# Two more landing places in ring slots, and a seventh product half a step earlier, in a spectral MLP kernel

## The chip, the cores and the metric

The kernel runs on one core of a Trainium2 chip. Its engines work in parallel, each through its own row of instructions in order, and wait for each other through semaphores: TensorE (PE in the profile, its weight loads PEld) multiplies, VectorE (DVE) and ScalarE (ACT) work element by element, GpSimd (POOL) does a few small powers, SyncE (SP) issues the transfers between the chip's main memory and on-chip memory. The metric is device time in microseconds (us) of one execution; the median of three runs is given. Below the chip is told only as the profile shows it.

## The reference

Two layers, each an FNet mixing (a Fourier transform over the hidden and the sequence axis, real part kept) and a spatial-shift MLP. S = 2048, D = 512, F = 1376, all float32:

```
def _A_ref(x, dft_seq_re, dft_seq_im, dft_hid_re, dft_hid_im):
    a = jnp.einsum("bsd,ed->bse", x, dft_hid_re)
    b = jnp.einsum("bsd,ed->bse", x, dft_hid_im)
    return jnp.einsum("ts,bse->bte", dft_seq_re, a) - jnp.einsum("ts,bse->bte", dft_seq_im, b)

def _B_ref(x, w1, w2, w3, w4):
    h = _gelu(_layernorm(x, axis=-1) @ w1)
    ...                                  # four column groups shifted by +1, -1, +2, -2 rows
    x1 = x + hs                          # hs: the shifted h @ w2
    return x1 + _gelu(_layernorm(x1, axis=-1) @ w3) @ w4

x = x + _A_ref(_layernorm(x, axis=-1), ...)
x = x + _B_ref(_layernorm(x, axis=-1), ...)
x = x + _A_ref(_layernorm(x, axis=-1), ...)      # layer 1 from here
x = x + _B_ref(_layernorm(x, axis=-1), ...)
```

## The kernel before

Every product of float32 matrices is made of three TensorE products of a high and a low part of each operand (mm3, lines 343 to 345: high by high, high by low, low by high). So every operand must be split: ScalarE casts a high part, VectorE subtracts it from the source to get the low part.

The transform over the sequence is done in four chunks c of 512 rows. Each chunk has an **x phase** and a **y phase** of eight blocks k. An x phase has 16 half-steps: in half-step 2k the block of the sequence matrix "plain k" is multiplied into the PSUM banks PC and PB (two banks, "a pair", each), in half-step 2k + 1 "half k" (one 128x512 part: the difference of the two rows of the same block) into PA. A y phase has for each k an item "by1" (into PC and PD) and one "by0" (into PB and PA). What a chunk leaves is copied out of PSUM and then multiplied with the hidden transform's matrices.

In layer 1 that second multiplication, for chunk c - 1, is spread over the x phase of chunk c (c = 1, 2, 3) as **seven products of half-size matrices, forms 0 to 6**, in place of eight (hid7). The left operands are sums of the four quarters (a11 ... a22 in the tiles imL, reL, s2, s3), split into a high part in one of two buffers hf[n % 2] (form_high, ScalarE, line 490) and a low part written in place (form_low, VectorE, line 494). The right operands are two blocks for each form, ready-made in main memory (hsd). The table HAT7 says in which half-step each form's products run: 5, 10, 11, 12, 13, 14, 15. Form n accumulates in PD[n % 2], and forms 0, 1, 3 and 6 start it anew. hid7_out adds what stands in PD to the result tiles (VectorE, line 567, the rows with "psd"), at the first half-step after the form's own, in form_outs; form 4 is added to two column halves at once (128x1024), the others are 128x512. So form 6, which starts PD[0] anew, needs form 4's sum to be done, and PD's first product of the y phase needs those of forms 5 and 6. The sums and splits of the left operands are hung on half-steps in the table "late" at the end of y_phase.

**How operands come in.** A list of *pieces* (transfers of 512 KB) is issued in order on SP's queue by issue_dma, each as soon as a *raw place* is free: four places, and two more (raw 4 and 5) for pieces of y phases and, in layer 1, of all that ahead_pieces lists. ahead_pieces sorts the pieces by the half-step in which they are due; a form's two are due one half-step ahead of it. A list of *items* is worked on in two stages by prefetch: stage one makes the difference where one is needed (VectorE, lines 281 and 285) and the high part (ScalarE, lines 279, 282, 286) in one of four slots of a *ring*, stage two the low part (VectorE, line 300). A form's item takes no slot: its products read the raw place. Stage one runs ahead of the products as far as slots are free and pieces are issued, in the order of the list, and stops at the first item whose piece has no place. The program is recorded in exactly the order in which these functions are called, so a place more shifts where an item's instructions stand on VectorE and ScalarE, relative to the forms' work and the rest.

A slot holds high and low parts of two rows (2 x 2 x 512 words). An item "half" uses the first row only, so in layer 1's x phases with c > 0, where odd slots hold "half" items, the second halves of slots 1 and 3 are unused.

**Beside it** a unit of layer 1's w4 is prepared in each x phase (w4_sums): loaded at half-step 2, four sums of 128x256 on VectorE and a cast on ScalarE at half-step 13, the low part and the transfer out to main memory at half-step 15.

The page's names: ring0f to ring3f are the differences in the four slots, imL and reL the forms' low parts, hf the high parts, rawr a form's block in its raw place, tmp the result tiles.

Of the kernel before, what the change touches and what calls it, by code (L numbers as in the profile page):

```python
# [8 lines left out]
F32 = mybir.dt.float32  # L9
# [10 lines left out]
CH = 512  # L20
# [3 lines left out]
DH = D // 2  # L24
# [14 lines left out]
BACK = {8: 0, 11: 2, 13: 4}  # L39
HORDER = ((1, 0), (0, 1), (1, 1), (0, 0))  # L40
XLEAD, YLEAD = 4.5, 3.5
HAT7 = (5, 10, 11, 12, 13, 14, 15)


@with_exitstack
def spectral_mlp_kernel(ctx: ExitStack, tc: tile.TileContext, x, ws, hs, w1, w2, w34, out):
# [41 lines left out]
    def at(name, word, *shape, dtype=F32R):  # L88
        return nc.alloc_sbuf_tensor_at(name, [P, *shape], dtype, offset=base + 4 * word).ap()
# [23 lines left out]
    raw_at += [at(f"raw{RAW + i}", word, 2, CH, dtype=F32) for i, word in enumerate((EXT + 4 * D, STG))]  # L113
    raw_in = [RAWS + i * 2 * CH for i in range(RAW)] + [EXT + 4 * D, STG]
    raw_in = [at(f"rawr{i}", word, 2, 2, DH) for i, word in enumerate(raw_in)]

    blk, blkf = {}, {}
    for i, word in (("11", H3), ("21", H3 + 4 * CH), ("12", RNG), ("22", RNG + 4 * CH)):
# [34 lines left out]
        return tmps[(count["tmp"] - 1) % len(tmps)]  # L153


    pieces, items, w_items, w_pieces, y_pieces = [], [], [], [], set()

    def piece(src, a=0, b=2):
        pieces.append((src, a, b))
# [10 lines left out]
    def ahead_pieces(c):  # L170
        order = [(2 * k - XLEAD, 0, (k,), ws[c, k][:, 2:4]) for k in range(NP)]
        order += [(t - 1, j, (h, j), hsd[h][j]) for h, t in enumerate(HAT7) for j in range(2)]
        for k in range(NP):
            order += [(2 * NP + 2 * k - YLEAD, i, (k, "y", i), ws[c, k][:, 2 - 2 * i : 4 - 2 * i]) for i in range(2)]
        order.sort(key=lambda o: o[:2])
        ids = {name: piece(src) for _, _, name, src in order}
        y_pieces.update(ids.values())
        return ids

    def form_items(step, ids):  # L180
# [5 lines left out]
    for layer in range(LAYERS):  # L186
        for c in range(NC):
            if layer == 0 and c == 0:
                for k in range(NP):
                    item("plain", piece(ws[c, k][:, 2:4]))  # L190
                    item("plain", piece(ws[c, k][:, 0:2]))
                continue
            if c and layer:
                ids = ahead_pieces(c)
                for k in range(NP):
                    form_items(2 * k, ids)
                    item("plain", ids[(k,)])
                    form_items(2 * k + 1, ids)
                    item("one", ids[(k,)], span=(0, 1))
                for k, kind in y_order():  # L200
                    item(kind, ids[k, "y", 0], ids[k, "y", 1])
                continue
            for k in range(NP):
                if c:
                    for h in range(NP):
                        if HAT[h] == k:
                            item("plain", piece(hs[HORDER[h % 4]]))
                p = piece(ws[c, k][:, 2:4])
                item("plain", p)
                item("one", p, span=(0, 1))  # L210
            ps = [(piece(ws[c, k][:, 2:4]), piece(ws[c, k][:, 0:2])) for k in range(NP)]
            y_pieces.update(i for p in ps for i in p)
            for k, kind in y_order():
                item(kind, *ps[k])
        for o in HORDER:
            item("plain", piece(hs[o]))
        w_items.append(len(items))
        for i in range(2):
            item("plain", piece(w1[i]), dest=w12[i])
        for i in range(2):  # L220
            item("plain", piece(w2[i]), dest=w12[2 + i])
        w_pieces.append(len(pieces))
# [18 lines left out]
    def issue_dma(upto=None):  # L241
        while state["dma"] < (state["load"] if upto is None else upto):
            i = state["dma"]
            free = [
                r
                for r, p in held.items()
                if (r < RAW or state["wide"] and i in y_pieces)
                and (p is None or all(n < state[stage] for n, stage in uses[p]))
            ]
            if not free:  # L250
                break
            src, a, b = pieces[i]
            r = min(free, key=lambda r: (-1 if held[r] is None else held[r], r))
            held[r] = i
            raws[i], place[i] = raw_at[r], r
            if uses[i][0][1] == "over":
                raws[i] = raw_in[r].bitcast(F32).rearrange("p i l w -> p i (l w)")
            nc.sync.dma_start(raws[i][:, a:b], src)
            state["dma"] += 1
            if i % 2 and i > 3:  # L260
                load_x()

    def stage_one():

        n = state["one"]
        kind, ids, (a, b), dest = items[n]
        issue_dma()
        if kind == "form":
            state["one"] += 1
            return  # L270
        if dest is None:
            dest = ring[state["made"] % RING]
            sums[n] = ringf[state["made"] % RING][:, :, 1]
            state["made"] += 1
        slots[n] = dest
        r = [raws[i] for i in ids]
        lo = sums.get(n)
        if kind == "plain":
            nc.scalar.copy(dest[:, a:b, 0], r[0][:, a:b])  # L279
        elif kind == "one":  # L280
            nc.vector.tensor_tensor(lo[:, 0], r[0][:, 1], r[0][:, 0], op=ALU.subtract)
            nc.scalar.copy(dest[:, 0, 0], lo[:, 0])  # L282
        else:
            i = 1 if kind == "by1" else 0
            nc.vector.tensor_tensor(lo, r[1][:, i : i + 1].broadcast_to([P, 2, CH]), r[0], op=ALU.subtract)  # L285
            nc.scalar.copy(dest[:, :, 0], lo)  # L286
        state["one"] += 1
        issue_dma()
# [285 lines left out]
    def x_phase(c, hook, seven=False, tiles=0):  # L574
# [2 lines left out]
        ready = []  # L577

        def form_steps(step):
            if seven and step in HAT7:  # L580
                ready.append(HAT7.index(step))
                hid7(ready[-1])

        def form_outs(step):
            while ready and HAT7[ready[0]] < step:
# [34 lines left out]
    def y_phase(c, hook, tiles=0):  # L620
# [32 lines left out]
        if tiles:  # L653
            for i, f in (
# [17 lines left out]
                (11, lambda: form_high(4)),  # L672
                (12, lambda: form_low(4)),
                (12, lambda: form_high(5)),
                (13, lambda: form_low(5)),
                (13, lambda: form_high(6)),
                (14, lambda: form_low(6)),
            ):
                late.setdefault(i, []).append(f)
            return  # L680
# [1188 lines left out]
    def w4_sums(k, i):  # L1869

        if i == 2:
            w4_bring(k)
        if i == (13 if layer else 10):
            w4_raw = w4_sumf[:, :, 0].rearrange("p (f h) w -> p h f w", f=2)
            a, b = (w4_raw[:, h] for h in range(2))
            s = w4_sumf[:, :, 1]
            add(s[:, 0], b[:, 0], b[:, 1])
            add(s[:, 1], s[:, 0], a[:, 0], ALU.subtract)
            add(s[:, 2], a[:, 0], b[:, 0], ALU.subtract)
            add(s[:, 3], a[:, 1], s[:, 1], ALU.subtract)  # L1880
            nc.scalar.copy(w4_sum[:, :, 0], s)
        if i == (15 if layer else 11):
            nc.vector.tensor_tensor(
                w4_sum[:, :, 1], w4_sumf[:, :, 1], w4_sum[:, :, 0].bitcast(F32), op=ALU.subtract
            )
            nc.sync.dma_start(w4s[k], w4_sum.bitcast(F32))
# [273 lines left out]
```

## Time and profile before

| | |
|---|---|
| runs | 1452.15, 1454.65, 1456.01 us; median 1454.65 |
| profiled execution | 1454.98 us, span of the instructions 1452.9 us |
| TensorE | busy 1420.9 us (98%), granted clock 0.996 on average |
| VectorE | busy 1204.9 us (83%) |
| ScalarE | busy 731.8 us (50%) |
| transfers | 324.05 MB on SP's queue, 66.9% of the 16 engines' time |

Busy time of TensorE is modelled and overlaps from one product to the next, so 98% does not mean that nothing can be gained; what can be seen is where it stands still, and what ended each such wait. In the part with layer 1's x phases c = 1 to 3 (780 to 1110 us from the start) the named waits of TensorE add up to 17.9 us. In a timeline each row has start and duration in us, engine, line, operation, the tile written and the tiles read, shapes and a count; a wait stands in brackets with what ended it.

### The profile page before, as it was taken

The page shows a single profiled execution, that of the slowest core. Times are in us where ns is not written, and L with a number is a line of the kernel's source. Part 1 is how long each engine was busy: PE and PEld are TensorE (multiplying, and loading weights), DVE is VectorE, ACT ScalarE, POOL GpSimd, SP SyncE. Part 2 cuts the span into 40 slices and gives each one's busy share as a digit, 9 for nine tenths or more (in the row PEclk, how much of TensorE's full clock was granted, in tenths as well). Part 3 has the DMA queues.
Part 4 walks back from the last instruction along what each step waited for, and adds up shares of the span by engine and source line. Part 5 has one row for each costly group of instructions (what it writes and reads, how often), then busy time and mean ns, then how long its engine had stood idle before and what let it go on. Part 6 is the DMA issues. An engine that isn't in the chain of part 4 may idle for free.

```text
span 1452.9 us, 18506 instructions
## 1 busy us (share of the span) xinstructions
PE 1420.9 (98%) x6681; PEld 1188.4 (82%) x6681; DVE 1204.9 (83%) x1725; ACT 731.8 (50%) x1020; POOL 76.6 (5%) x105
## 2 busy tenths in 40 slices
PE   9999999999999999998999989989989999999999
PEld 7888888888888888876888878878878888899887
DVE  7986998989978897667799878879879797897676
ACT  5663554445566654344555443444445666444342
POOL 2100000000002000000000000000000011000000
PEclk9999999999999999999999999999999999999999
DMA  7867657568645758877655577576687537586864
GB/s 247 274 204 234 200 173 261 173 200 296 226 133 161 268 214 282 329 251 263 232 173 190 203 256 225 187 269 222 207 294 240 173 102 275 165 250 217 320 205 163
DMA packets 145628, 325.24 MB, mean 224 GB/s; under 512 B 10624, under 2 KB 61568, under 8 KB 142848
## 3 DMA queue, kind: packets, MB, share of 16 engines
q1 hardware_dynamic: 145536, 324.05, 66.9%
q8 instruction: 53, 0.87, 0.2%
q14 instruction: 39, 0.32, 0.1%
HBM read 262.41 MB, written 61.60 MB: 223 GB/s over the span
## 4 chain that ended last, share of the span: by engine, by line
PE 83%; DVE 9%; DMA 4%; ACT 2%; issue 2%; SPq 0%; DVEq 0%; ACTq 0%
PE psd L343 8%; PE psd L345 8%; PE psd L344 8%; PE psa L343 7%; PE psa L344 7%; PE psa L345 7%; PE psb L344 6%; PE psb L343 6%; PE psb L345 6%; PE psc L344 6%; PE psc L345 6%; PE psc L343 6%; DVE ring L300 1%; DVE rest L567 1%; DMA raw<-in_ws 1%
## 5 line engine op out<-in xcount | busy, mean ns | idle before, releaser
L300 DVE TENSOR_TENSOR ring<-raw,ring 128x1024 fp32r<-128x1024 f32 x102 | 124.2, 1220 | 19.0 <-ACT ring L279 18.7
L279 ACT CAST ring<-raw 128x1024 fp32r<-128x1024 f32 x103 | 107.8, 1051 | 56.3 <-PE psd L345 25.6
L383 POOL TENSOR_TENSOR rs<-ve,mhalf 128x4 f32<-128x4 f32 x16 | 25.0, 1562 | 746.1 <-DVE nm L382 746.1
L343 PE MATMUL psd<-ring,ay 128*128 128x512 f32 x126 | 50.1, 398 | 7.8 <-DVE tmp L567 7.8
L300 DVE TENSOR_TENSOR ring<-ring1f,ring 128x512 fp32r<-128x512 f32 (+1 forms) x56 | 53.3, 952 | 2.9 <-ACT ring L282 2.9
L286 ACT CAST ring<-ring0f 128x1024 fp32r<-128x1024 f32 x28 | 29.5, 1053 | 50.5 <-DVE ring0f L285 50.2
L286 ACT CAST ring<-ring2f 128x1024 fp32r<-128x1024 f32 x28 | 29.6, 1056 | 48.8 <-DVE ring2f L285 48.8
L343 PE MATMUL psd<-rawr,hf 128*128 128x256 f32 x168 | 47.7, 284 | 5.8 <-issue 4.8
L343 PE MATMUL psc<-ring,ay 128*128 128x512 f32 x128 | 50.2, 392 | 2.0 <-ACT rr11f L608 1.7
L300 DVE TENSOR_TENSOR ring<-ring3f,ring 128x1024 fp32r<-128x1024 f32 (+1 forms) x50 | 49.3, 986 | 3.0 <-ACT ring L282 2.6
L362 POOL TENSOR_TENSOR rs<-ve,mhalf 128x2 f32<-128x2 f32 (+2 forms) x33 | 29.2, 886 | 426.6 <-DVE nb L361 407.6
L391 ACT ACTIVATE tmp<-xs,nb,rs 128x512 f32<-128x512 f32 x56 | 43.3, 810 | 15.8 <-POOL nb L363 12.6
L344 PE MATMUL psb<-ring,ay 128*128 128x512 f32 x128 | 50.3, 393 | 0.8 <-DVE ring L300 0.8
L343 PE MATMUL psb<-ring,ay 128*128 128x512 f32 x128 | 50.5, 394 | 0.0
L345 PE MATMUL psb<-ring,ay 128*128 128x512 f32 x128 | 50.1, 391 | 0.0
L345 PE MATMUL psd<-ring,ay 128*128 128x512 f32 x126 | 49.9, 396 | 0.0
L344 PE MATMUL psc<-ring,ay 128*128 128x512 f32 x128 | 49.8, 389 | 0.0
L345 PE MATMUL psc<-ring,ay 128*128 128x512 f32 x128 | 49.8, 389 | 0.0
L344 PE MATMUL psd<-ring,ay 128*128 128x512 f32 x126 | 49.8, 395 | 0.0
L344 PE MATMUL psa<-ring,ay 128*128 128x512 f32 x126 | 49.0, 389 | 0.0
L343 PE MATMUL psa<-ring,ay 128*128 128x512 f32 x126 | 49.0, 389 | 0.0
L345 PE MATMUL psa<-ring,ay 128*128 128x512 f32 x126 | 49.0, 389 | 0.0
(896 smaller groups left out, 4757.8 us busy)
## 6 DMA issues: line engine op xcount, KB each, us to landing
raw<-in_ws SPq DMA_DIRECT2D x183, 512.0 KB, 5.2
w4r<-w4d SPq DMA_DIRECT2D x44, 512.0 KB, 5.3
rawr<-hsd SPq DMA_DIRECT2D x42, 512.0 KB, 4.8
w3b<-w3d SPq DMA_DIRECT2D x10, 1792.0 KB, 9.3
raw<-in_hs SPq DMA_DIRECT2D x32, 512.0 KB, 4.0
w3d<-w3b SPq DMA_DIRECT2D x5, 1792.0 KB, 7.0
hsd<-hp SPq DMA_DIRECT2D x28, 256.0 KB, 2.4
x1d<-tmp SPq DMA_DIRECT2D x12, 512.0 KB, 7.4
```

Of the source, the lines that this page charges most:

```text
L279: nc.scalar.copy(dest[:, a:b, 0], r[0][:, a:b])
L286: nc.scalar.copy(dest[:, :, 0], lo)
L300: nc.vector.tensor_tensor(lo, src, hi.bitcast(F32), op=ALU.subtract)
L343: nc.tensor.matmul(o, lh, rh, start=first, stop=False, skip_group_check=more)
L344: nc.tensor.matmul(o, lh, rl, start=False, stop=False, skip_group_check=more)
L345: nc.tensor.matmul(o, ll, rh, start=False, stop=last, skip_group_check=more)
L362: nc.gpsimd.tensor_tensor(rs[:, :n], ve[:, :n], mhalf[:, 0, :n], op=ALU.pow)
L383: nc.gpsimd.tensor_tensor(rs, ve, mhalf[:, :, :2], op=ALU.pow)
L391: nc.scalar.activation(o, s, AF.Identity, bias=mr[2], scale=mr[1])
L567: nc.vector.tensor_tensor(o, a, b, op=op)
```

## The change

Five edits, all for layer 1's x phases with c > 0:

- Two raw places more (6 and 7): the unused halves of ring slots 1 and 3. Items "one" of these phases become "half" and get a tile of half the size, so that the rest of the slot is free. The two places take only blocks of forms whose half-step is below 13 (forms 0 to 3), and only after the first item of the phase has been used.
- HAT7's last entry: form 6's products run in half-step 14, directly after form 5's, and its two pieces are due at 13 with form 5's.
- form_steps takes the forms of one half-step in turn, and before a form's products it records the sum of a form that stands two back (form 4 before form 6).
- The left operand of form 6 is made in half-step 13: high part, then form 5's low part, then form 6's low part.
- w4's sums and cast move from half-step 13 to 14.

```diff
-HAT7 = (5, 10, 11, 12, 13, 14, 15)
+HAT7 = (5, 10, 11, 12, 13, 14, 14)
...
+    half_in = {i: both(f"ringh{i}", RNG + i * 4 * CH, 1, 2, CH) for i in (1, 3)}
+    raw_in += [at(f"rawr{RAW + 2 + i // 2}", RNG + i * 4 * CH + 2 * CH, 2, 2, DH) for i in (1, 3)]
+    raw_at += [raw_in[RAW + 2 + i].bitcast(F32).rearrange("p i l w -> p i (l w)") for i in range(2)]
...
+        early_pieces.update((ids[h, j], len(items)) for h in range(7) for j in range(2) if HAT7[h] < 13)
...
-                    item("one", ids[(k,)], span=(0, 1))
+                    item("half", ids[(k,)], span=(0, 1))
...
-                if (r < RAW or state["wide"] and i in y_pieces)
+                if (r < RAW or state["wide"] and (i in y_pieces if r < RAW + 2 else state["use"] > early_pieces.get(i, len(items))))
...
             if uses[i][0][1] == "over":
-                raws[i] = raw_in[r].bitcast(F32).rearrange("p i l w -> p i (l w)")
+                raws[i] = raw_at[r] if r > RAW + 1 else raw_in[r].bitcast(F32).rearrange("p i l w -> p i (l w)")
...
+            if kind == "half":
+                dest, whole = half_in[state["made"] % RING]
+                sums[n] = whole[:, :, 1]
...
-        elif kind == "one":
+        elif kind in ("one", "half"):
...
         def form_steps(step):
-            if seven and step in HAT7:
-                ready.append(HAT7.index(step))
-                hid7(ready[-1])
+            for h in range(7):
+                if seven and HAT7[h] == step:
+                    while ready and ready[0] < h - 1:
+                        hid7_out(ready.pop(0))
+                    ready.append(h)
+                    hid7(h)
...
                 (12, lambda: form_high(5)),
+                (13, lambda: form_high(6)),
                 (13, lambda: form_low(5)),
-                (13, lambda: form_high(6)),
-                (14, lambda: form_low(6)),
+                (13, lambda: form_low(6)),
...
-        if i == (13 if layer else 10):
+        if i == (14 if layer else 10):
```

How it moves the instructions. **VectorE, half-steps 9 and 10 of the x phase c = 1** (s2f and imLf are the forms' left operands, reL form 1's low part, s form 2's, ring3f and ring_206 or ringh_222 the half of k = 5 and its low part). Before:

```order
L567 TENSOR_TENSOR s2f<-reLf,s3f 128x1024
L567 TENSOR_TENSOR imLf<-imLf,reLf 128x4x256
L494 TENSOR_TENSOR reL<-reLf,hf_191 128x4x256
L567 TENSOR_TENSOR imLf<-reLf,s2f 128x4x256
L494 TENSOR_TENSOR s_186<-s2f,hf_190 128x1024
L281 TENSOR_TENSOR ring3f<-raw_209 128x512
L300 TENSOR_TENSOR ring_206<-ring3f,ring_206 128x512
```

and now:

```order
L574 TENSOR_TENSOR s2f<-reLf,s3f 128x1024
L288 TENSOR_TENSOR ringh3f<-raw_209 128x512
L307 TENSOR_TENSOR ringh_222<-ringh3f,ringh_222 128x512
L574 TENSOR_TENSOR imLf<-imLf,reLf 128x4x256
L501 TENSOR_TENSOR reL<-reLf,hf_191 128x4x256
L574 TENSOR_TENSOR imLf<-reLf,s2f 128x4x256
L501 TENSOR_TENSOR s_186<-s2f,hf_190 128x1024
```

The half of k = 5 and its low part have moved from behind form 2's low part to ahead of form 1's.

**VectorE, half-steps 13 to 15** (imL is form 5's low part, reL form 6's; psd_287 and psd_293 are PD[1], read for form 3's sum, psd_286 and psd_292 PD[0], read for form 4's; the first row before is the low part of plain 7, ring3f its half, ring0f and ring1f the y phase's first two items). Before:

```order
L300 TENSOR_TENSOR ring_204<-raw_213,ring_204 128x2x512
L494 TENSOR_TENSOR imL<-imLf,hf_191 128x4x256
L567 TENSOR_TENSOR w4sumf<-w4sumf 128x256 x4
L567 TENSOR_TENSOR tmp<-tmp,psd_287 128x2x256
L281 TENSOR_TENSOR ring3f<-raw_213 128x512
L285 TENSOR_TENSOR ring0f<-raw_209,raw_210 128x2x512
L300 TENSOR_TENSOR ring_206<-ring3f,ring_206 128x512
L285 TENSOR_TENSOR ring1f<-raw_209,raw_210 128x2x512
L300 TENSOR_TENSOR ring_200<-ring0f,ring_200 128x2x512
L300 TENSOR_TENSOR ring_202<-ring1f,ring_202 128x2x512
L494 TENSOR_TENSOR reL<-reLf,hf_190 128x4x256
L567 TENSOR_TENSOR tmp<-tmp,psd_286 128x1024
```

and now:

```order
L501 TENSOR_TENSOR imL<-imLf,hf_191 128x4x256
L501 TENSOR_TENSOR reL<-reLf,hf_190 128x4x256
L574 TENSOR_TENSOR tmp<-tmp,psd_293 128x2x256
L288 TENSOR_TENSOR ringh3f<-raw_211 128x512
L307 TENSOR_TENSOR ring_204<-raw_211,ring_204 128x2x512
L292 TENSOR_TENSOR ring0f<-raw_208,raw_210 128x2x512
L307 TENSOR_TENSOR ringh_222<-ringh3f,ringh_222 128x512
L292 TENSOR_TENSOR ring1f<-raw_208,raw_210 128x2x512
L307 TENSOR_TENSOR ring_200<-ring0f,ring_200 128x2x512
L574 TENSOR_TENSOR tmp<-tmp,psd_292 128x1024
L307 TENSOR_TENSOR ring_202<-ring1f,ring_202 128x2x512
L574 TENSOR_TENSOR w4sumf<-w4sumf 128x256 x4
```

Form 6's low part has moved from near the end to directly behind form 5's, plain 7's low part from the front to behind the half, and w4's sums and the low part of the y phase's second item from ahead of form 4's sum to behind it. Behind these rows both have ring2f, w4's low part, the statistics (c = 1 and 2) and the sums of forms 5 and 6; before, ring2f's low part stood among them too, and now it comes later.

**TensorE, the first products of form 6** (rawr is the form's block; in brackets what the instruction waits for). Before, behind the last PB product of k = 7:

```order
L343 MATMUL psb_283<-ring_204,ax_152 128x512
L344 MATMUL psb_283<-ring_204,ax_152 128x512
L345 MATMUL psb_283<-ring_204,ax_152 128x512
L343 MATMUL psd_286<-rawr_217,hf_190 128x256 [waits DMAHW5_49,DVE_49,Activation_49]
L344 MATMUL psd_286<-rawr_217,hf_190 128x256
```

and now, behind the last product of form 5:

```order
L352 MATMUL psd_293<-rawr_219,imL 128x256
L350 MATMUL psd_293<-rawr_219,hf_191 128x256
L351 MATMUL psd_293<-rawr_219,hf_191 128x256
L352 MATMUL psd_293<-rawr_219,imL 128x256
L350 MATMUL psd_292<-rawr_218,hf_190 128x256 [waits DMAHW4_49,DVE_49,Activation_49]
```

The PC and PB products of k = 7 now come behind form 6's, and its first product waits for a transfer, VectorE and ScalarE as before.

More of the change, by code (lines that the diff above doesn't have):

```diff
@@ L153, in tmp_tile @@
         return tmps[(count["tmp"] - 1) % len(tmps)]
-    pieces, items, w_items, w_pieces, y_pieces = [], [], [], [], set()
+    pieces, items, w_items, w_pieces, y_pieces, early_pieces = [], [], [], [], set(), {}
     def piece(src, a=0, b=2):
```

## The prediction

> **What bounds the kernel now.** I read the chain of waits first, then what TensorE waited for in the stretch that the change touches (layer 1, x phases of c = 1, 2, 3, 780 to 1110 us), then the timelines of TensorE, VectorE and ScalarE around each of these waits.
>
> ```profile
> PE 83%; DVE 9%; DMA 4%; ACT 2%; issue 2%; SPq 0%; DVEq 0%; ACTq 0%
> ```
>
> TensorE sets the end for 83% of the span. So what counts is each stretch in which it stands still, and an edit away from it costs or gains only through such a stretch. In the touched part there are these (engine, line, what ended the wait, us in total, times, longest):
>
> ```profile
> PE psd L343 <- DVE tmp L567: 7.8, 3, 3.2
> PE psd L343 <- issue: 4.8, 3, 2.0
> ...
> PE psd L345 <- DVE reL L494: 1.6, 3, 0.6
> ```
>
> Each comes once per phase. The columns below are start, duration, engine, line, operation, count, and in brackets the idle time before it:
>
> ```profile
> 857.15 0.40 PE L343 MATMUL psc<-ring,ax 128*128 128x512 f32 x1
> ...
> 862.05 0.36 PE L343 MATMUL psd<-rawr,hf 128*128 128x256 f32 x1 [2.00 <-issue]
> ...
> 865.00 0.40 PE L343 MATMUL psa<-ring,ax 128*128 128x512 f32 x1
> ...
> 871.62 0.80 PE L343 MATMUL psd<-ring,ay 128*128 128x512 f32 x1 [3.19 <-DVE tmp L567]
> ```
>
> 857.15 is the last PC/PB pair of half-step 14; 862.05 is form 6 (the seventh) in half-step 15; 865.00 the last PA pair; 871.62 the y phase's first product into PD. Two VectorE rows say what the two waits are:
>
> ```profile
> 860.74 1.21 DVE L567 TENSOR_TENSOR tmp<-tmp,psd 128x1024 f32<-128x1024 f32 x1
> ...
> 870.29 1.28 DVE L567 TENSOR_TENSOR tmp<-tmp,psd 128x512 f32<-128x512 f32 x2
> ```
>
> The 128x1024 add is the sum that takes form 4 out of PD[0] (hid7_out(4)); it ends at 861.95, and form 6, which starts PD[0] anew, begins 0.10 later. So the wait marked "issue" is for form 4's sum. The second row takes forms 5 and 6 out; it ends at 871.57, and PD's first y product follows. Phase c = 2 has the same pair:
>
> ```profile
> 965.72 1.22 DVE L567 TENSOR_TENSOR tmp<-tmp,psd 128x1024 f32<-128x1024 f32 x1
> 967.04 0.36 PE L343 MATMUL psd<-rawr,hf 128*128 128x256 f32 x1 [2.00 <-issue]
> ```
>
> Both waits are thus for VectorE's place in its own row of work, not for blocks from memory.
>
> **The change, first place: half-step 9 to 10.** Two more places let the items be staged earlier, so the half of block k = 5 (ringh3f and its low part) now stands on VectorE ahead of the low part of form 1, which TensorE already waits for:
>
> ```profile
> 826.00 0.69 DVE L281 TENSOR_TENSOR ring1f<-raw 128x512 f32<-128x512 f32 x1
> 827.43 0.69 DVE L300 TENSOR_TENSOR ring<-ring1f,ring 128x512 fp32r<-128x512 f32 x1 [0.74 <-ACT ring L282]
> ...
> 832.05 1.22 DVE L567 TENSOR_TENSOR imLf<-imLf,reLf 128x1024 f32<-128x1024 f32 x1
> 833.37 1.23 DVE L494 TENSOR_TENSOR reL<-reLf,hf 128x1024 fp32r<-128x1024 f32 x1
> ...
> 834.65 0.39 PE L345 MATMUL psd<-rawr,reL 128*128 128x256 f32 x1 [0.55 <-DVE reL L494]
> ```
>
> A half and its low part, back to back, cost 1.43 from start to start (826.00 to 827.43, ScalarE's cast between them) and 0.60 for the low part itself (the same operation, 855.52 to 856.12 below). So imLf moves from 832.05 to 834.08, form 1's low part from 833.37 to 835.40, and TensorE, which follows it without slack, waits 2.03 longer. Bounds: 0 if some slack hides it (none shows: there is a 0.55 wait already), 2.03 if none. I take 2.03, three times: **+6.1**. Later rows of VectorE do not give it back, since the next waits hang on TensorE's own form 4.
>
> **Second place: half-steps 13 to 15.** I count from T, ScalarE's cast of form 6's high part, which starts as form 4's last product reads that buffer:
>
> ```profile
> 843.14 1.05 ACT L490 CAST hf<-s3f 128x1024 fp32r<-128x1024 f32 x1 [1.18 <-PE psd L344]
> ...
> 852.97 1.05 ACT L490 CAST hf<-reLf 128x1024 fp32r<-128x1024 f32 x1 [3.62 <-PE psd L344]
> ```
>
> ```profile
> 844.22 1.23 DVE L494 TENSOR_TENSOR s<-s3f,hf 128x1024 fp32r<-128x1024 f32 x1 [0.58 <-ACT hf L490]
> 845.37 0.68 DVE L567 TENSOR_TENSOR tmp<-tmp,psd 128x512 f32<-128x512 f32 x1
> ...
> 851.65 1.55 DVE L567 TENSOR_TENSOR w4sumf<-w4sumf 128x256 f32<-128x256 f32 x4
> 853.12 0.68 DVE L567 TENSOR_TENSOR tmp<-tmp,psd 128x512 f32<-128x512 f32 x1
> 853.72 0.68 DVE L281 TENSOR_TENSOR ring3f<-raw 128x512 f32<-128x512 f32 x1
> 854.32 1.22 DVE L285 TENSOR_TENSOR ring0f<-raw,raw 128x1024 f32<-128x1024 f32 x1
> 855.52 0.69 DVE L300 TENSOR_TENSOR ring<-ring3f,ring 128x512 fp32r<-128x512 f32 x1
> 856.12 1.22 DVE L285 TENSOR_TENSOR ring1f<-raw,raw 128x1024 f32<-128x1024 f32 x1
> 857.26 1.22 DVE L300 TENSOR_TENSOR ring<-ring0f,ring 128x1024 fp32r<-128x1024 f32 x1
> 858.46 1.23 DVE L300 TENSOR_TENSOR ring<-ring1f,ring 128x1024 fp32r<-128x1024 f32 x1
> ```
>
> With the change form 6's low part stands right behind form 5's, before everything else of this stretch. It cannot start before ScalarE has made the high part (844.22 - 843.14 = 1.08 after the cast's start), so VectorE idles until T + 1.08, and behind it queue, in the order of the rows: form 6's low 1.15, form 3's sum 0.60, the half of k = 7 0.60, the low part of plain 7 1.15 (now behind a cast that itself comes after form 6's), ring0f 1.20, the half's low 0.60, ring1f 1.14, ring0's low 1.20, then form 4's sum 1.21 and 0.10 to TensorE. Form 6 begins at T + 10.03. Before it was 862.05 - 852.97 = T + 9.08. So the products were moved up half a step, and the sum that they need got 0.95 later.
>
> What covered that wait does so no longer: the PC/PB pair of k = 7 (862.05 - 2.00 - 857.15 = 2.90) stood before form 6 and now stands behind it. PB ends at T + 10.03 + 2.95 (862.05 to 865.00) + 2.90 = T + 15.88. Slot 2 of the ring is free only then, and ring2f, first in VectorE's queue behind w4's sums, waits for it; behind it stand w4's low part, the statistics and the two sums that PD's first y product needs.
>
> ```profile
> 868.55 1.28 DVE L377 BATCH_NORM_STATS2 st<-tmp 128x6 f32<-128x512 f32 x2
> ```
>
> ring2f 1.15, w4's low 1.15, the statistics 1.74 (868.55 to 870.29), the sums and TensorE 1.33 (870.29 to 871.62): PD starts at T + 21.25 where it was T + 18.65. That is +2.60; c = 2 shows equal waits (2.00 above, 3.18 below), so again +2.60. In c = 3 these statistics are not there:
>
> ```profile
> 1062.95 1.05 ACT L490 CAST hf<-reLf 128x1024 fp32r<-128x1024 f32 x1 [3.62 <-PE psd L344]
> ...
> 1081.30 0.50 PE L343 MATMUL psd<-ring,ay 128*128 128x512 f32 x1 [1.45 <-DVE tmp L567]
> ```
>
> T + 19.51 against T + 18.35, +1.16. Together **+6.4**. The sums of forms 5 and 6 stay late because of their place behind ring2f.
>
> **Edits at nothing.** w4's four sums (851.65 to 853.12, 1.5) stood ahead of form 4's sum and now stand behind it, in VectorE's wait for PB, which hides them; without that wait they would delay ring2f by 1.5. On SP's queue form 5's second block is now issued only when form 4's second half is through (about T) and the y blocks follow it:
>
> ```profile
> DMA to landing us min/median/max: 3.5/5.0/5.5
> ```
>
> It lands by T + 5.5, form 5 is done about 1.4 later, T + 6.9, and form 6 waits until T + 10.03 anyway. If that cover were gone it would cost up to 2.8 per phase. Form 1's blocks go out before w4's loads instead of after them: nothing waits for either.
>
> **The clock.** A long wait has a second price (columns end with granted clock, DMA share, GB/s):
>
> ```profile
> 976.49 0.50 PE L343 MATMUL psd<-ring,ay 128*128 128x512 f32 x1 [3.18 <-DVE tmp L567]
> 976.40:980.40 4.00, 3.91 (x11) 3.07 (x12) 2.67 (x4) 1.23 (x2) 1.23 (x1) 0.60 0.83 252
> ...
> 680.33 0.79 PE L343 MATMUL psd<-b,w3b 128*128 128x512 f32 x1 [2.67 <-DVE rest L567]
> 680.00:683.00 3.00, 2.67 (x6) 2.15 (x7) 1.64 (x5) 3.00 (x7) 0.00 (x0) 0.54 0.15 59
> ...
> 661.48 0.50 PE L343 MATMUL psa<-b,w3b 128*128 128x512 f32 x1 [3.05 <-DVE rest L567]
> 661.00:664.00 3.00, 2.52 (x11) 2.11 (x12) 1.78 (x4) 3.00 (x6) 0.00 (x0) 1.00 0.12 46
> ```
>
> A wait of 3.18 was followed by 4.00 us at 0.60, 1.6 lost; one of 2.67 by 3.00 at 0.54, 1.4; one of 3.05 by none. Now form 5 would end at T + 4.2 and form 6 wait 5.8: I count a spell of 1.5 in each phase, 4.5. The PD wait in c = 1 and 2 becomes 21.25 - 15.88 less the PA pair and y's first PC pair (865.00 to 871.62 less the 3.19, 3.4 with overlapping ends), some 2.0 to 2.6: I give a spell there even odds, 1.5 for both together. The spells of c = 1 and 2 at PD, 1.5 each, go. Net **+3.0**, between -3.0 (no spell) and +4.5.
>
> The Trainium skill, "TensorE: Matmul & The Clock Gate", Part 1 (the HAM clock gate), has the array at half rate after an idle window of about 3.4 us on a free-running count. The trace halves the clock after 2.67 and 3.18 already, so it is less strict than that. By the page's rule, as an estimate, a wait of 5.8 holds a whole window 0.7 of the time and the PD wait never: 3.2 - 3.0, and the total would be some 2.8 lower.
>
> **Sum.** 6.1 + 6.4 + 3.0 = 15.5 on the profiled execution's 1454.98 (span 1452.9 and 2.1 around it): 1470.5. The median of the runs is 0.3 lower: **1470.1**.
>
> **Rivals.** (a) The clock stays up, since form 5's late second block breaks the long wait in two: 1470.1 - 6.0 = 1464.1. For it: the 3.05 case; against: two others. (b) Form 1's low part is not late: 1464.0. Against it: the 0.55 wait that stands there now. (c) On the other side: the sum of form 4 is done while form 5's products run, so that form 6 follows without a wait. That takes form 4's sum ending by T + 4.2 instead of T + 9.9; then the waits of 4.8 and 7.8 and the 3.0 of slow clock go, the 6.1 of form 1 stays, and it ends at 1454.65 - 15.6 + 6.1 = 1445. For it: VectorE is idle right before T + 1.08, so its rows could move up if they did not hang on form 6's cast; against it: form 6's low part stands first and seven others between it and the sum, and the engine took its rows one behind the other in all the lists above. (d) Form 6's second block comes about 1.5 after T + 11.5, when it is wanted (an estimate; a landing took up to 5.5 above, and loads of c = 3 share the queue), and PD's wait is followed by slow clock in c = 1 and 2: 1470.1 + 3 x 1.5 + 1.5 = 1476.
>
> **How the numbers follow.** Forecast 0.58, (a) 0.14, (b) 0.10, (c) 0.05, (d) 0.08; 0.05 for a mixture of small terms that ends level. The measurement of this kernel can tell about 0.3% (4.4 us) from no change. Slower 0.89, within 0.05, faster 0.06. The range of 8 in 10 goes from just below (a) and (b), 1461, to (d), 1476.
>
> **What would show it.** Right: form 1's wait at half-step 10 grows from 0.55 to about 2.6; form 6 begins 0.1 after the 128x1024 sum, and PC/PB come behind it; between form 5 and form 6 some 5.8 of idle or two pieces of it; PD's first y product again right behind the sum of form 6, after ring2f that waited for PB. Wrong: form 6 following form 5 within 1 us, PD's wait gone, or form 1's low part at its old distance from the half-step's start.

## The result, and the profile after

| | before | changed |
|---|---|---|
| median (runs) | 1454.14 us (1452.15 to 1456.01, 4) | 1470.22 us (1468.11 to 1471.20, 4) |
| profiled execution, span | 1454.98, 1452.9 | 1469.96, 1467.9 |
| granted clock of TensorE, mean | 0.996 | 0.992 |

The ratio is 1.0109, its 95% interval 1.0091 to 1.0127: 1.1% slower. The prediction was 1470.1.

The chain of waits of the changed kernel still ends on TensorE for four fifths of the span; VectorE's share went from 9% to 11%:

```profile
PE 80%; DVE 11%; ACT 3%; issue 2%; DMA 2%; POOL 0%; SPq 0%; DVEq 0%; ACTq 0%; POOLq 0%
```

What TensorE waited for between 780 and 1130 us (us in total, times, longest):

```profile
PE psd L350 <- issue: 13.0, 5, 3.7
PE psd L350 <- DVE tmp L574: 7.8, 4, 2.7
PE psd L352 <- DVE reL L501: 7.6, 3, 2.6
```

The third row is form 1's low part: 7.6 where it was 1.6. The first two hold what form 5, form 6 and PD's first y product wait for, 20.8 in place of 12.6. The "issue" and "tmp" names mix all three, so they have to be taken apart in the timeline. First VectorE, phase c = 1, around form 1's low part:

```profile
831.34 0.68 DVE L288 TENSOR_TENSOR ringh3f<-raw 128x512 f32<-128x512 f32 x1
832.77 0.69 DVE L307 TENSOR_TENSOR ringh<-ringh3f,ringh 128x512 fp32r<-128x512 f32 x1 [0.74 <-ACT ringh L289]
...
834.63 1.23 DVE L501 TENSOR_TENSOR reL<-reLf,hf 128x1024 fp32r<-128x1024 f32 x1
```

The half of k = 5 and its low part stand ahead of it, 1.43 from start to start, as the prediction had it. TensorE's rows of the phase show who waits:

```profile
835.91 0.39 PE L352 MATMUL psd<-rawr,reL 128*128 128x256 f32 x1 [2.52 <-DVE reL L501]
...
858.73 0.36 PE L350 MATMUL psd<-rawr,hf 128*128 128x256 f32 x1 [1.53 <-issue]
...
865.60 0.55 PE L350 MATMUL psd<-rawr,hf 128*128 128x256 f32 x1 [3.68 <-issue]
...
879.50 0.50 PE L350 MATMUL psd<-ring,ay 128*128 128x512 f32 x1 [2.68 <-DVE tmp L574]
```

These are form 1, form 5, form 6 and PD's first y product. ScalarE's cast of form 6's high part, the T of the prediction, starts at 855.72, and VectorE goes on from there:

```profile
855.72 1.05 ACT L497 CAST hf<-reLf 128x1024 fp32r<-128x1024 f32 x1 [4.56 <-PE psd L351]
```

```profile
856.80 1.23 DVE L501 TENSOR_TENSOR reL<-reLf,hf 128x1024 fp32r<-128x1024 f32 x1 [4.38 <-ACT hf L497]
857.94 0.68 DVE L574 TENSOR_TENSOR tmp<-tmp,psd 128x512 f32<-128x512 f32 x1
...
864.29 1.22 DVE L574 TENSOR_TENSOR tmp<-tmp,psd 128x1024 f32<-128x1024 f32 x1
...
874.14 1.23 DVE L292 TENSOR_TENSOR ring2f<-raw,raw 128x1024 f32<-128x1024 f32 x1 [6.04 <-PE psb L352]
...
878.17 1.28 DVE L574 TENSOR_TENSOR tmp<-tmp,psd 128x512 f32<-128x512 f32 x2
```

VectorE stands idle for 4.38 until the cast is made, and behind form 6's low part run seven more rows before form 4's sum (the 128x1024 row), which ends at 865.51; form 6 follows 0.09 later, at T + 9.88. ring2f waits 6.04 for PB, and the sums of forms 5 and 6 come behind it. Form 5's 1.53 is new and is not in the prediction: the 128x512 row at 857.94 is form 3's sum out of PD[1], into which form 5 goes on adding; it ends at 858.62, and form 5 begins at 858.73. The sum stands behind form 6's low part now.

The rows by stretch of c = 1 (window, its length, busy time and count of TensorE, its weight loads, VectorE, ScalarE and GpSimd, granted clock, DMA share, GB/s):

```profile
862.00:868.00 6.00, 2.40 (x11) 2.43 (x12) 5.97 (x9) 1.62 (x2) 0.00 (x0) 0.73 0.93 322
868.00:874.00 6.00, 6.00 (x28) 5.45 (x27) 0.10 (x1) 2.71 (x4) 0.00 (x0) 0.70 0.72 263
874.00:880.00 6.00, 3.32 (x15) 2.47 (x14) 5.83 (x12) 2.71 (x5) 1.66 (x2) 1.00 0.45 186
880.00:885.00 5.00, 5.00 (x23) 4.10 (x23) 5.00 (x5) 2.11 (x2) 0.64 (x1) 1.00 0.64 138
```

The slow clock comes with form 6's wait (0.73, 0.70); behind PD's wait at 879.50 it stays at 1.00. It came once more where the prediction has none: behind form 1's wait of 2.52 in c = 1 the granted clock from 837 to 841 is 0.57, so that 1.7 of these 4 us are lost. Behind form 1's waits of c = 2 and 3 it stayed up.

### The profile page after: what moved, and what is told of

Same layout as the page of the kernel before. It is cut to its first block, busy times and chain, and to the rows that moved or that the text cites. A ratio compares the mean times of both kernels' runs of the same rounds, so it can differ in the third digit from the quotient of the medians.

```text
span 1467.9 us, 18501 instructions
## 1 busy us (share of the span) xinstructions
PE 1426.3 (97%) x6681; PEld 1195.0 (81%) x6681; DVE 1203.9 (82%) x1725; ACT 732.9 (50%) x1020; POOL 76.3 (5%) x105
## 4 chain that ended last, share of the span: by engine, by line
PE 80%; DVE 11%; ACT 3%; issue 2%; DMA 2%; POOL 0%; SPq 0%; DVEq 0%; ACTq 0%; POOLq 0%
PE psd L350 8%; PE psd L352 8%; PE psd L351 8%; PE psa L350 6%; PE psa L351 6%; PE psa L352 6%; PE psb L351 6%; PE psb L352 6%; PE psb L350 6%; PE psc L351 6%; PE psc L350 6%; PE psc L352 6%; DVE ring L307 2%; DVE rest L574 1%; DMA hs<-in_hs 1%
## 5 line engine op out<-in xcount | busy, mean ns | idle before, releaser
L350 PE MATMUL psd<-rawr,hf 128*128 128x256 f32 x168 | 51.1, 304 | 15.3 <-issue 13.0
L351 PE MATMUL psd<-rawr,hf 128*128 128x256 f32 x168 | 50.3, 300 | 0.0
L350 PEld LDWEIGHTS psd<-rawr,hf 128*128 128x128 f32 x168 | 34.8, 207 | 18.1 <-issue 10.5
L292 DVE TENSOR_TENSOR ring2f<-raw,raw 128x1024 f32<-128x1024 f32 x28 | 34.1, 1219 | 17.8 <-PE psb L352 15.8
```

The source lines that it names most:

```text
L350: nc.tensor.matmul(o, lh, rh, start=first, stop=False, skip_group_check=more)
L351: nc.tensor.matmul(o, lh, rl, start=False, stop=False, skip_group_check=more)
```

## The experiments

Each runs beside the kernel before on the same chip: its median there was 1454.73 (first four), 1455.09 (next four) and 1455.35 (last two). "..." in a diff leaves code out.

**1. The changed kernel without the two places.**

```diff
-                    item("half", ids[(k,)], span=(0, 1))
+                    item("one", ids[(k,)], span=(0, 1))
...
-    raw_at += [raw_in[RAW + 2 + i].bitcast(F32).rearrange("p i l w -> p i (l w)") for i in range(2)]
```

> The changed kernel without its two extra raw places (items are 'one' again, six places): on VectorE the half of k = 5 stands behind form 2's low part again, the rows of half-steps 13 to 15 stay as in the change. My theory: form 1's wait falls from 2.5 to 0.55 in each phase, 3 x 2.0 = 6.0 us less, 1464.2. Rival (the places help the second part, where blocks come earlier because of them): form 5 and form 6 wait longer for blocks and the time stays at 1470 or rises.

Measured 1465.01 (1464.73 to 1466.83), ratio 1.0072 (1.0057 to 1.0087). TensorE's row at form 1's low part:

```profile
833.95 0.39 PE L351 MATMUL psd<-rawr,reL 128*128 128x256 f32 x1 [0.55 <-DVE reL L500]
```

It is back at the 0.55 of before, and the waits of forms 5, 6 and of PD are within 0.2 of the changed kernel's. The places cost 5.2 here, by the span too (1467.9 - 1462.7), and 5.9 by form 1's named waits (7.6 against 1.7); the first term of the sum holds. The spells of slow clock are not the same ones: there is none behind form 1 here, but one behind each of PD's waits of 2.67 and 2.68 (clock 0.57 from 875 to 879, 0.59 from 984 to 988).

**2. The places alone, in the kernel before.** HAT7, the table of the left operands and w4's half-step as before.

> The kernel before with only the two places added (form 6 in half-step 15, w4's sums at 13, the left operands as before). My theory: form 1's wait grows from 0.55 to 2.5 in each phase, everything behind it shifts with TensorE: 1454.1 + 6.0 = 1460.1, less up to 1.5 where ring2f waited for a y block in c = 1 and 3. Rival: places alone are harmless, since the row of work is the same, and the whole 15 us come from the seventh product: 1454.

Measured 1464.75 (1461.44 to 1467.01), ratio 1.0066 (1.0048 to 1.0084). So the places are harmful by themselves. The median is 4.7 above what was expected; the profiled execution, 1461.44, is nearer. In its span of 1459.4 TensorE waits for these, among others, in the touched part:

```profile
PE psd L352 <- DVE reL L501: 7.8, 3, 2.8
...
PE psc L350 <- ACT rr11f L618: 1.6, 1, 1.6
PE psc L350 <- ACT imLf L618: 1.3, 2, 0.7
```

Form 1 takes 6.2 more than before, and the first PC product of y phases 1.0 more (2.9 against 1.9): 7.2, of which 6.5 shows in the span (1459.4 - 1452.9). The 3.3 between this execution and the median go with the clock: its mean was 0.996 here and 0.991 to 0.993 in the three longer runs, and 0.003 of 1460 us is, as an estimate, 4.4.

**3. Form 4's sum recorded before form 5's products**, so that VectorE has it directly behind form 3's sum.

```diff
-                    while ready and ready[0] < h - 1:
+                    while ready and (ready[0] < h - 1 or ready[0] == h - 1 == 4):
```

> The change with form 4's sum recorded before form 5's products, so that on VectorE it stands right behind form 3's sum. With T as the start of form 6's high cast, my theory: the sum ends at T + 4.1, form 6 follows form 5 as soon as its blocks are there (T + 5.7 to T + 8), PB ends at T + 12.4, PD's first y product comes at T + 18.0 (c = 3: T + 16.2) instead of T + 23.8, 22.6 and 20.9: 15 us less, 1455, up to 4.5 more if the clock falls after PD's wait of 3. Rival (form 6 is held by its blocks, not by the sum): it begins no earlier than T + 9 and the time stays above 1467.

Measured 1461.48 (1457.51 to 1467.10, 10 runs), ratio 1.0048 (1.0031 to 1.0065). Form 6 no longer waits for the sum. In c = 1 only its second block holds it up, and PD's wait has grown from 2.68 to 3.24:

```profile
862.70 0.39 PE L350 MATMUL psd<-rawr,hf 128*128 128x256 f32 x1 [0.56 <-DMA rawr<-hsd]
...
873.60 0.50 PE L350 MATMUL psd<-ring,ay 128*128 128x512 f32 x1 [3.24 <-DVE tmp L574]
```

With T = 854.43 in this execution PD starts at T + 19.17, where the changed kernel has T + 23.78. So the second term rests on the place of form 4's sum, as the prediction said. But the time is 6.5 above the 1455 of the expectation, 2.0 above it with all of the 4.5 that was allowed for the clock. PD comes 1.1 to 1.3 later than expected in each phase (T + 19.17, 19.07 and 17.46), 3.5 in all: it waits for sums that still stand behind ring2f, w4's low part and the statistics. The rest goes with the clock, whose mean is 0.998 in the three shortest runs and 0.992 or 0.993 in the four longest.

**4. Also the sums of forms 5 and 6 ahead of half-step 15's staging.**

```diff
+            if seven and last:
+                form_outs(2 * k + 1)
             s = stream()
```

> As the kernel with form 4's sum first, and also forms 5's and 6's sums recorded ahead of ring2f, w4's low part and the statistics. My theory: PD's first y product is released at about T + 13.8 and follows the first PC pair without a wait (about T + 15), the second y block may wait 1 to 2 for ring2's low part: 1448 to 1452, below the kernel before although form 1's 6 us are still paid. Rival (VectorE as a whole is the bound there, and whatever is moved ahead makes something else late by as much): no better than 1455.

Measured 1455.68 (1453.23 to 1457.08, 10 runs), ratio 1.0006 (0.9997 to 1.0016): level with before, 3.7 above the upper end of what was expected. PD waits no more. The largest named waits that are left:

```profile
PE psd L352 <- DVE reL L501: 7.6, 3, 2.6
PE psd L350 <- issue: 3.1, 2, 1.5
PE psd L350 <- DMA rawr<-hsd: 2.5, 5, 1.0
PE psb L351 <- DVE ring L307: 2.1, 1, 2.1
PE psd L350 <- DVE tmp L574: 1.5, 1, 1.5
```

The 3.1 and the last 1.5 are form 5's three waits of 1.53, which I had left out: hidden in the changed kernel by form 6's, they count as soon as that is gone. The next four take the rest apart.

**5. Experiment 4 without the places** (edit as in 1).

> Both sums recorded early (form 4's before form 5's products, forms 5 and 6's before half-step 15's staging), but without the two places, so that the half of k = 5 and its low part go back behind form 2's low part. Theory: the places cost what form 1's low part waits, 2.5 less 0.55, about 2.0 per phase, also when the rest of the change costs nothing: 1455.7 - 6 = 1449.7, form 1's waits back at 0.5 to 0.6, form 5's 1.5 unchanged. Rival: the places bring forms' blocks earlier, and without them the blocks of forms 5 and 6 land later still; then waits on DMA of some us appear and it stays within 1454 to 1456.

Measured 1448.42 (1446.15 to 1449.15), ratio 0.9950 (0.9938 to 0.9962). 7.3 less than experiment 4, somewhat more than the 6 expected; form 1's waits are at 0.55, 0.54 and 0.65, and the waits on blocks are 2.9 in all where they were 2.5. The rival falls.

**6. Experiment 4 with form 3's sum ahead of the low parts too.**

```diff
-            if seven and last:
+            if seven and k > 5:
                 form_outs(2 * k + 1)
             s = stream()
```

> The kernel with both sums early, and with form 3's sum as well ahead of form 5's and 6's low parts; the two places stay. Theory: form 5 waits 1.53 per phase only because form 3's sum stands behind form 6's low part, and that wait counts now that nothing later covers it: 1455.7 - 4.5 = 1451.2, no wait ahead of form 5. Rival: form 5's second block is late anyway (it could not be told from the sum, since both come at about the same time), so that most of the 1.5 turns into a wait on DMA: 1454 to 1456.

Measured 1452.72 (1449.29 to 1455.33, 12 runs), ratio 0.9980 (0.9970 to 0.9991). 3.0 of the 4.5 came. Form 5 starts without a wait in c = 1 and 2, so the 1.53 was the sum. But TensorE now stands still half-way through form 5. In c = 1 (T is 854.26 here):

```profile
856.89 0.28 PE L352 MATMUL psd<-rawr,imL 128*128 128x256 f32 x1
860.06 0.58 PE L350 MATMUL psd<-rawr,hf 128*128 128x256 f32 x1 [2.89 <-DMA rawr<-hsd]
...
860.66 0.41 PE L352 MATMUL psd<-rawr,imL 128*128 128x256 f32 x1
```

imL, form 5's low part, is read before the wait and behind it, so the wait is for form 5's second block, which comes at T + 5.80. Both readings were partly right: the sum held form 5's first half, and behind it stood the late second block of the rival. The waits on blocks are 8.6 in all, where they were 2.5. By named waits alone this kernel should not be faster than that of experiment 4 (18.6 in all against 17.5), and the two profiled executions differ by 1.1 only; which part of the 3.0 is a matter of the clock (the runs with a mean of 0.998 took 1449.3 to 1452.1, the others 1452.1 to 1455.3) stays open.

**7. Experiments 5 and 6 together.**

> Both of the two edits before together: all sums early and no places. Theory, the two add up: 1455.7 - 6.0 - 4.5 = 1445.2, faster than before by 9, with no named wait over 1 us in the x phases. Rival: the waits move on to the y phase's items or to the forms' blocks (a sum of 2 to 4 us of new waits on DMA or on the low parts of ring tiles): 1447 to 1450.

Measured 1445.01 (1443.98 to 1446.19), ratio **0.9930 (0.9918 to 0.9942)**: 10 us faster than before, as expected. Named waits:

```profile
PE psd L349 <- DMA rawr<-hsd: 5.8, 3, 2.0
PE psd L351 <- DVE reL L500: 1.8, 3, 0.7
PE psb L350 <- DVE ring L306: 1.6, 1, 1.6
```

The time is that of the theory, but not for its whole reason: a wait of 5.8 for form 5's second block is left that the theory did not name and the rival did.

```profile
857.39 0.39 PE L349 MATMUL psd<-rawr,hf 128*128 128x256 f32 x1 [1.92 <-DMA rawr<-hsd]
```

Without the places that block is there 1.0 sooner in c = 1 (T = 852.57, T + 4.82) and 1.2 in c = 2, but 0.3 later in c = 3. So in two of the phases the places cost twice, once by VectorE's order and once by that block.

**8. The changed kernel with w4's sums back in half-step 13.**

```diff
-        if i == (14 if layer else 10):
+        if i == (13 if layer else 10):
```

> The changed kernel with w4's sums back in half-step 13, all else as changed. Theory: VectorE's row between form 6's cast and form 4's sum is full, so the 1.47 of w4's four sums go on form 6's start in full: form 5 starts 1.5 later, form 6 at T + 11.4 instead of T + 9.9, PD's first y product 1.5 later in each phase: 1470.2 + 4.4 = 1474.6, which says that moving w4's sums was worth 4.4 to the changed kernel. Rival: the sums fit into VectorE's idle time before T + 1.08 or are taken up by its wait for PB: 1470.2.

Measured 1477.89 (1474.79 to 1480.93), ratio 1.0155 (1.0137 to 1.0173). Form 5 and form 6 of c = 1, with T = 855.37:

```profile
859.84 0.52 PE L350 MATMUL psd<-rawr,hf 128*128 128x256 f32 x1 [2.99 <-issue]
867.67 0.55 PE L350 MATMUL psd<-rawr,hf 128*128 128x256 f32 x1 [3.21 <-issue]
```

Form 5 is 1.46 later against T, form 6 2.42 (T + 12.30): 0.95 more than the 1.47 that the sums themselves take, since the low part of plain 7 now also waits 0.86 for its cast. The mean clock is 0.988 against 0.992. Moving w4's sums helped the changed kernel by 7.7 in the medians (1477.89 - 1470.22) and 6.4 in the spans (1474.3 - 1467.9), more than the 4.4 expected.

**9. The kernel before with the sums of forms 2 to 5 ahead of staging, nothing else.** Two lines like those of experiment 6, in each of the half-steps 12 to 15.

> The kernel before with nothing of the change, only the sums of forms 3, 4 and 5 recorded ahead of the staging of their half-step in half-steps 13 to 15 (form 6's last sum stays behind w4's low part and the statistics). Theory: form 4's sum ends 2.35 earlier (the low parts of ring1 and of form 6 go behind it), so that form 6's first product no longer waits, but its third, which reads the low part, does, by about 1.1; PD's first y product hangs on ring2f's pieces, w4's low part and the statistics, which do not move, and takes over what form 6 gives back: 1454 to 1455, as before. Rival: PD moves up with form 6, and the kernel gains 2.0 to 4.5: 1450 to 1452.

Measured 1454.69 (1450.76 to 1457.68, 12 runs), ratio 0.9992 (0.9981 to 1.0002): no change, as expected. In c = 1 and 2 form 6's first product no longer waits, its third waits 1.64 and 1.65, and PD's wait is where it was (in c = 3 the third waits 1.04, and the y phase's first PC product 2.37 in place of PD):

```profile
861.19 0.38 PE L345 MATMUL psd<-rawr,reL 128*128 128x256 f32 x1 [1.64 <-DVE reL L494]
...
870.64 0.50 PE L343 MATMUL psd<-ring,ay 128*128 128x512 f32 x1 [3.18 <-DVE tmp L567]
```

**10. Experiment 7 with form 6's products back in half-step 15.**

```diff
-HAT7 = (5, 10, 11, 12, 13, 14, 14)
+HAT7 = (5, 10, 11, 12, 13, 14, 15)
...
             if seven and k > 5:
-                form_outs(2 * k + 1)
+                form_outs(2 * k + 1 + last)
```

> The kernel with all three sums early and without the places, with one thing put back: form 6's products run in half-step 15 again, behind the PC and PB products of k = 7, and its blocks are due one half-step later. The sums of forms 5 and 6 follow form 6's products. Theory: what is left of TensorE's waits in the kernel it is made from is form 6 waiting 1.9 to 2.0 per phase for its first block, 5.8 in all; with the PC/PB pair between the forms the block has 2.9 longer and the wait is gone; ring2f stands ahead of the sums again, but these end at about T + 15.7 and PD's first product is due at about T + 15.5, so 0 to 0.6 in all: 1445.0 - 5.8 = 1439 to 1441. That would say that running the product earlier was worth nothing, only the places of the sums were. Rival: the blocks come one half-step later because they are due later, and ring2f, which waited for its pieces until T + 10.9 before the change, holds the sums and PD back by 2 or more per phase: 1445 or above, and the early product has a worth of its own.

Measured 1454.02 (1449.81 to 1457.98, 12 runs), ratio 0.9995 (0.9983 to 1.0007). The theory falls by 13 us or more. The expectation put the waits of 1.9 to 2.0 down to form 6's first block; they were for form 5's second one. They are gone in all three phases, and the list of pieces in the kernel gives a reason:

```
order += [(t - 1, j, (h, j), hsd[h][j]) for h, t in enumerate(HAT7) for j in range(2)]
...
order.sort(key=lambda o: o[:2])
```

Pieces that are due in the same half-step are sorted by j, first blocks ahead of second ones. With both forms in half-step 14, form 6's first block is issued ahead of form 5's second; here it is issued behind it. (The list alone was not changed in any run.) But the y phase's first PC product waits 5.03, 3.50 and 2.26. ScalarE in c = 1 and TensorE's row:

```profile
867.54 1.04 ACT L292 CAST ring<-ring2f 128x1024 fp32r<-128x1024 f32 x1 [2.99 <-DVE ring2f L291]
868.50 1.06 ACT L617 COPY imLf<-psc 128x512 f32<-128x512 f32 x2
```

```profile
869.13 0.79 PE L349 MATMUL psc<-ring,ay 128*128 128x512 f32 x1 [5.03 <-ACT imLf L617]
```

The products into PC were done at about 858.5, ten us before, but the copy that empties PC stands behind ring2f's cast in ScalarE's row, and ring2f was not begun until 866.23. In experiment 7 the row reads the other way:

```profile
865.42 1.07 ACT L617 COPY imLf<-psc 128x512 f32<-128x512 f32 x2
...
867.56 1.06 ACT L292 CAST ring<-ring2f 128x1024 fp32r<-128x1024 f32 x1
```

With form 6 early, ring2f is recorded behind the copies of PC and PB. So putting form 6 back costs 9.0 (1454.02 - 1445.01) once the sums are early. How much of that is the product itself is not shown: the three waits for the copy add up to 10.8, and a late form 6 with these copies ahead of ring2f's cast was not tried. Without the early sums the early product does not pay (experiment 1: 10.3 above the kernel before). The order of ScalarE's row fits what the Trainium skill says in "PSUM — Partial Sum Buffer", section "Engine vs sequencer instructions": ScalarE's and VectorE's queues are strict first in, first out. Here a copy whose input was long ready stood behind a cast that waited 2.99 and then took 0.96.

## Why the prediction came out

**Form 1, +6.1: right.** Its three waits grew by 6.0 (7.6 against 1.6). Without the places they are back (experiment 1), with the places alone they are there (experiment 2). The cost of the places as a whole is 5.2 to 7.7, by experiments 1, 5 and 7 against the same kernels with the places (alone, in experiment 2, 10.0).

**Form 6 and PD, +6.4, and the clock, +3.0: right in place, and in sum by some luck.** Form 6 was forecast at T + 10.03 and came at T + 9.88, 9.89 and 9.89 in the three phases. These rows of c = 2 and 3, with 865.60 and 879.50 above, carry it:

```profile
976.22 0.36 PE L350 MATMUL psd<-rawr,hf 128*128 128x256 f32 x1 [3.49 <-issue]
...
988.97 0.50 PE L350 MATMUL psd<-ring,ay 128*128 128x512 f32 x1 [2.67 <-DVE tmp L574]
...
1085.78 0.35 PE L350 MATMUL psd<-rawr,hf 128*128 128x256 f32 x1 [2.79 <-issue]
...
1096.78 0.50 PE L350 MATMUL psd<-ring,ay 128*128 128x512 f32 x1 [0.93 <-DVE tmp L574]
```

```profile
966.33 1.05 ACT L497 CAST hf<-reLf 128x1024 fp32r<-128x1024 f32 x1 [4.58 <-PE psd L351]
...
1075.89 1.05 ACT L497 CAST hf<-reLf 128x1024 fp32r<-128x1024 f32 x1 [4.57 <-PE psd L351]
```

PD starts at T + 23.78, 22.64 and 20.89, where before it was 18.65, 18.54 and 18.35: 5.13 + 4.10 + 2.54 = 11.8. That holds the waits and the slow clock behind form 6 together; 6.4 and 4.5 were forecast, 10.9. Taking the forecast waits away leaves 2.5, 1.5 and 1.4 for the slow clock, so it lasted longer in c = 1 than the 1.5 assumed. The spells behind PD's wait, given even odds, did not come (waits of 2.68 and 2.67, clock 1.00), and the 3.0 of before went. 6.0 + 11.8 - 3.0 = 14.8, and the span grew by 15.0. That these come so close is luck: 1.5 too much was forecast behind PD and 0.9 too little behind form 6; the spell behind form 1 in c = 1, 1.7, was not forecast at all; and against it stand 0.7 by which phase c = 1 began sooner (form 1's high cast at 828.76, before at 829.46) and 0.5 less of one wait in the last y phase (0.3, before 0.8).

**Form 5: half read, at no cost in the total.** The prediction put its delay on the second block (T + 5.5) and had form 5 end at T + 6.9. Its start it did not look at, and that is held by the sum of form 3, standing behind form 6's low part in the very list that the prediction made; who writes PD[1] next was not asked. Form 5 started at T + 3.01 in each phase. The second block came about as forecast: in c = 3 form 5 waits 0.73 for it, to T + 5.41, and form 5 is done at T + 6.2, 6.4 and 7.1. PD, through form 6, felt neither. With the cover gone, the sum's wait cost 3.0 to 3.4 (experiment 4 against 6, 5 against 7), and behind it the block's wait appeared, 5.8 in experiment 7.

**Rival (c), 1445 if form 4's sum is done in time: its condition was tried, its price was wrong.** Experiment 3 meets the condition and gives 1461.5, since the 7.8 at PD did not go with it, but stayed at 7.5 in the touched part (3.24, 3.14 and 1.11). That wait belongs to the sums of forms 5 and 6. Rival (a) needed the clock to stay up; the wait did come in two pieces (1.53 and 3.68, by the sum and not by the block), and the clock fell to 0.70 to 0.73 all the same; rival (b) is refuted by form 1's rows; (d) would have needed a late second block of form 6 and spells at PD, and there were none.

**w4's sums at nothing: right for the changed kernel**, where they lie in VectorE's wait for PB (6.04); left in half-step 13 they would have cost 6.4 to 7.7 (experiment 8), more than their 1.5 per phase.

So the change lost its 15 us by the order of the rows on VectorE: with the sums of forms 3 to 6 at the front and without the places it beats the kernel before by 0.7%, and takes 25 us less than as it was made. Neither part does it alone: the early sums without the early product leave the time as before (experiments 9 and 10), the early product without the early sums costs 10.3 (experiment 1).

## What to carry to other kernels

Moving a product earlier moves also what it waits for: list what frees its accumulator, find where that row stands on its engine, and move it along, since an engine's row is worked off in its order. For every row that goes behind a late one, ask who reads its output next, hidden waits too; a wait that another covers today is the first to show when that one is mended. More places to land data in can be harmful when the order of recording follows from them: they let staging run ahead of work that TensorE already waits for. And where two groups of transfers become due at the same step, look how the list sorts them. To tell whose wait a row is, read the rows on both sides of it: the tile that they share names the product.

## What was not expected of the hardware

The clock fell after form 6's waits of 3.68, 3.49 and also 2.79 (windows of the changed kernel, c = 2 and 3), and not after PD's of 2.68 and 2.67, nor in c = 1 of experiment 3 after 3.24:

```profile
976.00:982.00 6.00, 5.78 (x30) 5.60 (x31) 2.68 (x6) 1.44 (x2) 0.00 (x0) 0.72 0.91 313
...
1085.00:1091.00 6.00, 5.22 (x28) 5.12 (x29) 3.24 (x6) 1.04 (x1) 0.00 (x0) 0.72 0.91 339
```

Experiment 3, with PD's product at 873.60:

```profile
872.00:878.00 6.00, 4.40 (x19) 3.67 (x20) 5.96 (x10) 2.04 (x3) 2.29 (x2) 1.00 0.88 268
```

Nor do the shorter waits draw a line. In experiment 7 the clock fell after form 5's 1.92 (0.53 from 858 to 861.5), in the changed kernel once after form 1's 2.52, in experiment 1 after PD's 2.67 and 2.68; in experiment 6, c = 2, it stayed at 1.00 after 3.08. The length of a wait alone does not decide it. The Trainium skill, "TensorE: Matmul & The Clock Gate", Part 1 (the HAM clock gate), gives half rate after an idle window of about 3.4 us, and has the window free-running. That the same length can go either way agrees with a free-running count, but falls after 1.92 and 2.79 do not agree with 3.4.

The spread of runs fits a clock that goes either way: kernels with a wait of 3 us or so spread over 6 to 10 us (experiments 3, 6, 9 and 10: 9.6, 6.0, 6.9 and 8.2), those whose longest waits are 2.6 or less over 2 to 4 (experiments 4, 5 and 7: 3.9, 3.0 and 2.2; 5 to 12 runs each). In experiment 3 the mean clock goes with the time, from 0.998 in the shortest runs to 0.993 in the longest; 0.005 of 1460 us is, as an estimate, 7.3 of the spread of 9.6. In experiment 4, with little spread, it does not (0.994 to 0.996). That the clock is the cause of this spread was not tried.
